# Attention scores of every unit as plain float32, the two heads on two halves of the TensorE rows

## The chip, the cores and the metric

The kernel runs on one core of a Trainium2 chip. The metric is the time of one execution on the device in microseconds (us). A core has TensorE (PE, matrix products; PEld is its weight load), VectorE (DVE), ScalarE (ACT), GpSimd (POOL) and SyncE (SP, which here issues most DMAs). Products are accumulated in PSUM, eight banks of 512 float32 words in each of 128 partitions; everything else lies in SBUF.

## The reference, cut to what matters

Four sequences of 768 tokens, eight heads of 64 go through a sparse attention, and its output through two feed-forward networks. A token attends to the 96 tokens up to itself and to the first 8 tokens.

```python
scores = scale * np.matmul(q, k.transpose(0, 1, 3, 2)) + bias   # bias: -slope * distance
scores = np.where(keep, scores, -1000000000.0)
a = softmax(scores);  x = np.matmul(a, v)
h = (x @ w1) * (x @ w2) @ w3;  x = h @ w_out                    # first network
h = x @ w_in;  out = (h * np.cos(h)) @ w_out2                   # second network
```

## The kernel before, in words

**Units.** The attention is cut into 96 units. A unit is 128 query tokens of one sequence for a pair of heads; its keys are a window of 232 columns (`WIN`): the 128 tokens of the tile, the 96 before it and the 8 global ones. Units run in an order written out by hand, three tiles (`TPB`) of a head pair, then the next pair; four pairs make a block of 384 tokens (`TB`), of which there are eight.

**A unit's steps**, each a function called with the unit's number: load (`a_load` or `a_load_plain`, and `a_load_v` for the values), scores on PE (`a_scores`), bias and row maximum on DVE (`a_max`, L569), exponential on ACT (`a_exp`), the norm on ACT or POOL (`a_norm`), transposition on PE (`a_transpose`) and its copy on ACT (`a_tcopy`), product with the values on PE (`a_values`, L635; from block 1 on for three units at once) and the result's copy (`a_out`).

**Scores in two ways.** Units 0 to 21 (`PLAIN`) are plain float32: both heads' queries and keys lie on partitions 0 to 63, and each head is one product over 64 rows (L541), which the trace shows as two passes. The other 74 units are split: the array is loaded twice, on both halves of the partitions (`a_load`, L496). ACT rounds it to float32r (`a_split_hi`, L517, tile `hh`), and DVE subtracts to get the rests (`a_split_lo`, L524 and L527): the lower halves of the queries' rows hold the value, the upper the rest, and `kl` holds the keys' rests. A head is then two accumulated products over 128 rows (L549, L553), one pass each. The scores of a unit, both heads in one bank, go to one of two buffers of the PSUM pool `p_s`, opened with `bufs` 2 (L285).

**Stages.** First the product W of two weight matrices is built in 16 chunks (L854, plain float32, 512 columns), while the weights of everything are decoded from 64-bit words (`decode`, on ACT at L330 and L332, on DVE at L336, L340, L348) and units 0 to 13 run in between. Then, in 96 slots (`for j`, `for i`), block j goes through the first network: a slot has two groups of 12 matmuls of 384 columns each (`up` or `down`, by `mm3`, L392 to L394), and unit `sl + 14` (`LEAD`) is put between them. In slot order: the load of a unit two or three ahead, `a_scores(n)`, the values of earlier units, the split of unit n + 2, maximum, decoding, exponential, the first group of 12 matmuls, transposition of unit n - 1, norm, the second group of 12. The last 14 slots have no attention. From about 640 us on the second network runs alone (`hidden`, `gate`, `project`).

Within an engine's queue the work is done in program order; loads by SP are issued in the order written, too, and wait there for their buffer.

Of the kernel before, what the change touches and what calls it, by code (L numbers as in the profile page):

```python
# [8 lines left out]
F32 = mybir.dt.float32  # L9
# [4 lines left out]
ALU = mybir.AluOpType  # L14
# [9 lines left out]
LOC, GLB = 96, 8  # L24
NPV = LOC + GLB
WIN = 128 + NPV
QK_W = 2 * 128 + 2 * WIN
TB = 384
NB1 = NT // TB
TPB = TB // 128  # L30
# [4 lines left out]
NB2 = NT // TB2  # L35
M2 = DF2 // 128
LEAD = 14
PLAIN = 22
INV2PI = 0.15915494309189535
C1 = 6.28125  # L40
C2 = 0.0019353071795864769
# [18 lines left out]
def general(ctx, tc, dram, misc, ident, nv, mm_out, packed):  # L60
# [7 lines left out]
    def attention(ctx):  # L68
# [35 lines left out]
        with tc.For_i(0, B, 1) as b:  # L104
            for p in range(NPAIR):
                for e in range(2):
# [5 lines left out]
                    for t in range(nt):  # L112
                        n = bass.ds(b * (nt * NPAIR) + (t // TPB) * UPB + p * TPB + t % TPB, 1)
                        c = slice(t * 128, (t + 1) * 128)
                        k0 = 256 + e * WIN
                        nc.sync.dma_start(
                            out=qt[:, c], in_=a_qk[n, 0:64, e * 128:(e + 1) * 128]
                        )
                        nc.sync.dma_start(out=kt[:, c], in_=a_qk[n, 0:64, k0:k0 + 128])
                        nc.sync.dma_start(out=vt[:, t, :], in_=a_v[n, :, e * 64:(e + 1) * 64])  # L120
                    xo = work.tile([64, S], F32, name="g_x")
                    for t in range(nt):
# [141 lines left out]
def fused(ctx, tc, a_qk, a_v, w3p, wo1p, w1p, w2p, winp, wo2p, n_global, n_local, out):  # L264
# [221 lines left out]
        p, i = divmod(r, TPB)  # L486
        return j, p, i, (TPB * j + i) % (S // 128)

    plain = {}
    qk_raw, v_raw, hh, kl, es, sts, pts, xps, xT = {}, {}, {}, {}, {}, {}, {}, {}, {}  # L490

    def a_load(n):
        if not PLAIN <= n < NU:
            return
        t = attn.tile([128, QK_W], F32, tag="qk", name="qk", bufs=2)
        nc.sync.dma_start(out=t, in_=a_qk[n])  # L496
        qk_raw[n] = t

    def a_load_plain(n, queue=None):

        if not 0 <= n < PLAIN:
            return
        t = plain[n] = attn.tile([128, QK_W], F32R, tag="hh", name="hh")[0:64].bitcast(F32)
        (queue or nc.sync).dma_start(out=t, in_=a_qk[n, 0:64])

    def a_load_v(n):
        if not 0 <= n < NU:
# [2 lines left out]
        nc.sync.dma_start(out=t.rearrange("p a b -> p (a b)"), in_=a_v[n])  # L510
        v_raw[n] = t

    def a_split_hi(n):
        if not PLAIN <= n < NU:
            return
        hh[n] = attn.tile([128, QK_W], F32R, tag="hh", name="hh")
        nc.scalar.copy(out=hh[n], in_=qk_raw[n])  # L517

    def a_split_lo(n):
        if not PLAIN <= n < NU:  # L520
            return
        r, t = qk_raw.pop(n), hh[n]
        kl[n] = attn.tile([128, 2 * WIN], F32R, tag="kl", name="kl")
        nc.vector.tensor_tensor(  # L524
            out=kl[n], in0=r[:, 256:], in1=t[:, 256:].bitcast(F32), op=ALU.subtract
        )
        nc.vector.tensor_tensor(  # L527
            out=t[64:128, :256], in0=r[64:128, :256], in1=t[64:128, :256].bitcast(F32),
            op=ALU.subtract,
        )  # L530

    s_ps = {}

    def a_scores(n):
        if not 0 <= n < NU:
            return
        s_ps[n] = p_s.tile([128, 2, WIN], F32, tag="s", name="s_ps")
        if n in plain:
            t = plain.pop(n)
            for e in range(2):  # L540
                nc.tensor.matmul(  # L541
                    s_ps[n][:, e, :], lhsT=t[:, e * 128:(e + 1) * 128],
                    rhs=t[:, 256 + e * WIN:256 + (e + 1) * WIN], start=True, stop=True,
                )
            return
        t, l = hh.pop(n), kl.pop(n)
        for e in range(2):
            q = t[:, e * 128:(e + 1) * 128]
            nc.tensor.matmul(  # L549
                s_ps[n][:, e, :], lhsT=q, rhs=t[:, 256 + e * WIN:256 + (e + 1) * WIN],  # L550
                start=True, stop=False,
            )
            nc.tensor.matmul(  # L553
                s_ps[n][:, e, :], lhsT=q, rhs=l[:, e * WIN:(e + 1) * WIN],
                start=False, stop=True,
            )

    def a_max(n):
# [187 lines left out]
    with tc.manual_schedule():  # L746
# [81 lines left out]
            for _ in range(n):  # L828
                next(steps_left, None)

        a_load_plain(0, nc.scalar)
        a_scores(0)
        nc.vector.memset(pt_ps, 0.0)
        steps_b = biases(tp)
# [3 lines left out]
        for i in range(21):  # L838
            decode(1)
            if i == 0:  # L840
                a_load_plain(1)
                a_load_v(0)
            if i == 4:
                nv = next(steps_b)
            elif i >= 6:
                dists = dists or next(steps_b)
        W_ps = {}
        for c, (h, k) in enumerate(chunks):
            n = c - 1 if c < 2 * M1 - 1 else -9
            if k == 0:  # L850
                W_ps = {m: p_mm.tile([128, 512], F32, tag="mm", name="mm") for m in range(4)}

            def wmm(m):
                nc.tensor.matmul(  # L854
                    W_ps[m], lhsT=wt["w3", c][:, m * 128:(m + 1) * 128], rhs=wt["wo1", k],
                    start=k == 0, stop=k == M1 - 1,
                )
                if k == M1 - 1:
                    t = wt["W", 4 * h + m] = wts.tile(
                        [128, 2, 512], F32R, tag="Wb" if h else "Wa", name="W", bufs=4  # L860
                    )
                    nc.scalar.copy(out=t[:, 0, :], in_=W_ps[m])
                    nc.vector.tensor_tensor(  # L863
                        out=t[:, 1, :], in0=W_ps[m], in1=t[:, 0, :].bitcast(F32), op=ALU.subtract
                    )

            a_load(n + 3)
            a_load_v(n + 1 if n >= 0 else -1)
            if c < 4:
                bias_heads(*dists, range(2 * c, 2 * c + 2))  # L870
            elif c == 4:
                tp.release()
            if n > 0:
                a_scores(n)
            if n >= 0:
                a_load_plain(n + 2)
            a_values(n - 2)
            a_max(n)
            decode(1)
            a_out(n - 2)  # L880
            a_split_hi(n + 2)
            a_exp(n)
            decode(1)
            a_split_lo(n + 2)
            wmm(0)
            wmm(1)
            if c in (2, 3) or c == 2 * M1 - 1:

                wmm(2)
                wmm(3)  # L890
            a_transpose(n - 1)
            a_tcopy(n - 1)
            a_norm(n, True, lambda: decode(1)) if n >= 0 else decode(2)
            decode(2 if c < 8 else 3)
            if not (c in (2, 3) or c == 2 * M1 - 1):
                wmm(2)
                wmm(3)
# [17 lines left out]
        for j in range(NB1):  # L915
            for i in range(UPB):
# [3 lines left out]
                if last and i == 0:  # L920
                    attn.release()
                    w2p_ = pool("w2p", 6)
                a_load(n + 3)
                if last:
                    if i < 3:
                        late_load("in", i)
# [4 lines left out]
                    if i == 4:  # L931
                        x2_load(0, w2p_, "x2in")
                a_scores(n)
                a_load_plain(n + 2)
                if (n - 2) % TPB == TPB - 1:
                    for u in range(n - 1 - TPB, n - 1):
                        a_values(u)
                if n > LEAD + 1:
                    a_load_v(n - 1)
                a_split_hi(n + 2)  # L940
                if 1 <= i <= M1:
                    up_mult(j, i - 1)
                    up_hi(j, i - 1)
# [9 lines left out]
                    up_lo(j, i - 1)  # L953
                a_exp(n)
                a_out(n - 2)
                a_split_lo(n + 2)
                if i < M1:
                    up(j, i, "a")
                    up_copy(j, i)
# [130 lines left out]
def _layout(q, k, v, w3, w_out, w1, w2, w_in, w_out2):  # L1090

    import numpy as np

    nt = S // 128
    qk = np.zeros((NU, 128, QK_W), np.float32)
    vv = np.zeros((NU, 128, 2, 128), np.float32)
    for n in range(NU):
        j, r = divmod(n, UPB)
        p, i = divmod(r, TPB)
        b, t = divmod(TPB * j + i, nt)  # L1100
        lo = t * 128
        for e in range(2):
            h = 2 * p + e
            for half in (slice(0, 64), slice(64, 128)):
                qk[n, half, e * 128:(e + 1) * 128] = q[b, h, lo:lo + 128].T
                w = qk[n, half, 256 + e * WIN:256 + (e + 1) * WIN]
                w[:, :128] = k[b, h, lo:lo + 128].T
                if t:
                    w[:, 128:128 + LOC] = k[b, h, lo - LOC:lo].T
                    w[:, 128 + LOC:] = k[b, h, :GLB].T  # L1110
            c = slice(e * 64, (e + 1) * 64)
            vv[n, :, 0, c] = v[b, h, lo:lo + 128]
            if t:
                vv[n, :LOC, 1, c] = v[b, h, lo - LOC:lo]
                vv[n, LOC:NPV, 1, c] = v[b, h, :GLB]

    def cols(w):
        kk, f = w.shape[0] // 128, w.shape[1] // 128
        return np.ascontiguousarray(
            w.reshape(kk, 128, f, 128).transpose(2, 1, 0, 3).reshape(f, 128, kk * 128)  # L1120
        )

    def words(w):
        return np.ascontiguousarray(w).view(np.int64)

    w3t = np.ascontiguousarray(w3.T).reshape(M1, 128, 2, 512).transpose(2, 0, 1, 3)
    return {
        "a_qk": qk,
        "a_v": vv.reshape(NU, 128, 256),
        "w3p": words(w3t),  # L1130
        "wo1p": words(w_out.reshape(M1, 128, DM)),
        "w1p": words(cols(w1)),
        "w2p": words(cols(w2)),
        "winp": words(cols(w_in)),
        "wo2p": words(w_out2.reshape(M2, 128, DM)),
    }
# [24 lines left out]
```

## Time and profile before

| | us |
|---|---|
| median of 3 runs | 1170.43 |
| lowest and highest run | 1169.32, 1174.7 |
| the profiled execution | 1168.78 |
| its span | 1167.0 |
| PE busy | 1138.3 |
| weight loads (PEld) busy | 985.5 |
| DVE busy | 753.8 |
| ACT busy | 593.9 |
| POOL busy | 112.3 |

Busy time is time in which an engine had an instruction of the program at work; the engines run beside each other. Matmuls are pipelined: a pass starts before the last one has left the array, so that the distance of two starts says what a pass costs, and its own duration does not. A row of the timeline has the start, the duration, engine, line, operation, tiles (out<-in), shape, and how many instructions are merged in it; a number in brackets is idle time before it and what ended it.

### The profile page before, as it was taken

To read this page: it belongs to the slowest core of one execution; us is meant where nothing else is said; L and a number is where in the kernel's file an instruction comes from. 1 tells how busy PE (TensorE), PEld (TensorE's weight loads), DVE (VectorE), ACT (ScalarE), POOL (GpSimd) and SP (SyncE) were. 2 spreads that over 40 slices of the span, in tenths; PEclk is the share of its full clock that TensorE was granted. 3 is DMA by queue.
4 is the path that set the end of the run, shared out by engine and by line. 5 is a ranking of instruction groups with operands and counts; after the bars stand their busy time and mean duration, and the time that the engine had idled before them with its cause. 6 is when DMAs were issued, how large, how long until landed. Compare 5 with 4: busy or idle time off the path is not lost.

```text
span 1167.0 us, 17288 instructions
## 1 busy us (share of the span) xinstructions
PE 1138.3 (98%) x6178; PEld 985.5 (84%) x6178; DVE 753.8 (65%) x1696; ACT 593.9 (51%) x1309; POOL 112.3 (10%) x197
## 2 busy tenths in 40 slices
PE   5999999999999999999999999999999999999997
PEld 2455899999999999999999888888888888888885
DVE  7797786767676555555344766666666666666664
ACT  6997786666666555555444533333333333333332
POOL 0000001121112111111132300000000000000000
PEclk9899899999999999999999999999999999999999
DMA  8875686575654424343156302002003003000001
GB/s 267 249 227 179 213 298 215 168 222 158 206 169 152 134 88 141 90 151 95 57 173 210 117 1 89 20 1 89 20 1 96 14 1 102 7 1 36 1 1 39
DMA packets 64783, 131.12 MB, mean 112 GB/s; under 512 B 6576, under 2 KB 27312, under 8 KB 64688
## 3 DMA queue, kind: packets, MB, share of 16 engines
q1 hardware_dynamic: 57648, 117.03, 31.2%
q0 software_dynamic: 6528, 12.58, 3.7%
q8 instruction: 51, 0.84, 0.3%
q14 instruction: 44, 0.36, 0.1%
q10 hardware_dynamic: 512, 0.32, 0.1%
HBM read 102.64 MB, written 27.26 MB: 111 GB/s over the span
## 4 chain that ended last, share of the span: by engine, by line
PE 91%; ACT 3%; DMA 2%; DVE 2%; issue 1%; ACTq 0%; SPq 0%; DVEq 0%
PE mm L392 11%; PE mm L394 11%; PE mm L393 11%; PE o_ps L394 7%; PE h_ps L393 7%; PE o_ps L393 7%; PE h_ps L392 7%; PE o_ps L392 7%; PE h_ps L394 7%; PE x_ps L635 3%; PE mm L854 3%; PE pt_ps L608 2%; PE s_ps L553 1%; PE pt_ps L610 1%; PE s_ps L549 1%; DMA raw<-in_winp 1%
## 5 line engine op out<-in xcount | busy, mean ns | idle before, releaser
L1012 ACT ACTIVATE r<-r 128x512 f32<-128x512 f32 x96 | 60.7, 632 | 149.0 <-DVE r L1008 149.0
L1021 ACT CAST g<-r 128x512 fp32r<-128x512 f32 x96 | 59.6, 621 | 139.5 <-DVE r L1017 139.5
L601 POOL TENSOR_SCALAR e<-e,st 128x232 f32<-128x232 f32 x148 | 72.0, 498 | 499.5 <-DVE st L593 479.3
L517 ACT CAST hh<-qk 128x720 fp32r<-128x720 f32 x74 | 58.7, 794 | 118.4 <-PE s_ps L553 113.3
L1014 DVE SCALAR_TENSOR_TENSOR r<-r 128x512 f32<-128x512 f32 x96 | 66.4, 692 | 70.0 <-ACT r L1012 69.9
L1022 DVE TENSOR_TENSOR g<-r,g 128x512 fp32r<-128x512 f32 x96 | 66.5, 692 | 66.0 <-ACT g L1021 66.0
L392 PE MATMUL mm<-xT,wA 128*128 128x384 f32 x256 | 90.6, 354 | 2.3 <-DVE W L863 2.3
L569 DVE CUSTOM_DVE_ANT_0 e<-s_ps,bias 128x232 f32<-128x232 f32 (+1 forms) x192 | 65.5, 378 | 42.3 <-PE s_ps L553 38.9
L580 ACT ACTIVATE e<-e,top 128x232 f32<-128x232 f32 (+1 forms) x192 | 89.3, 468 | 2.3 <-DVE top L569 2.2
L392 PE MATMUL mm<-ab,W 128*128 128x384 f32 x256 | 89.8, 351 | 0.0
L392 PE MATMUL mm<-xT,wB 128*128 128x384 f32 x256 | 89.5, 350 | 0.0
L394 PE MATMUL mm<-xT,wA 128*128 128x384 f32 x256 | 86.9, 340 | 0.0
L393 PE MATMUL mm<-xT,wA 128*128 128x384 f32 x256 | 86.7, 338 | 0.0
L394 PE MATMUL mm<-xT,wB 128*128 128x384 f32 x256 | 86.2, 337 | 0.0
L394 PE MATMUL mm<-ab,W 128*128 128x384 f32 x256 | 86.2, 337 | 0.0
L393 PE MATMUL mm<-ab,W 128*128 128x384 f32 x256 | 85.9, 336 | 0.0
L393 PE MATMUL mm<-xT,wB 128*128 128x384 f32 x256 | 85.8, 335 | 0.0
L1005 DVE SCALAR_TENSOR_TENSOR r<-kt,h_ps 128x512 f32<-128x512 int32 x96 | 65.7, 684 | 28.5 <-ACT kt L1003 28.1
L1003 ACT ACTIVATE kt<-h_ps 128x512 int32<-128x512 f32 x96 | 57.2, 596 | 34.8 <-PE h_ps L394 34.8
L678 DVE TENSOR_TENSOR ab_f<-mm,a_sb 128x384 f32<-128x384 f32 x64 | 35.5, 555 | 55.8 <-PE mm L394 55.8
L1008 DVE SCALAR_TENSOR_TENSOR r<-kt,r 128x512 f32<-128x512 int32 x96 | 66.4, 692 | 3.3
L854 PE MATMUL mm<-wo,w 128*128 128x512 f32 x128 | 63.8, 632 | 4.5 <-DVE wo L348 4.5
(191 smaller groups left out, 3004.3 us busy)
## 6 DMA issues: line engine op xcount, KB each, us to landing
qk<-in_a_qk SPq DMA_DIRECT2D x74, 360.0 KB, 3.1
v<-in_a_v SPq DMA_DIRECT2D x96, 128.0 KB, 2.9
x2s<-x2t SPq DMA_DIRECT2D x32, 384.0 KB, 3.0
raw<-in_w3p SPq DMA_DIRECT2D x16, 512.0 KB, 5.2
raw<-in_winp SPq DMA_DIRECT2D x16, 512.0 KB, 4.3
late_w<-x SPq DMA_DIRECT2D x32, 256.0 KB, 2.1
raw<-in_wo2p SPq DMA_DIRECT2D x16, 512.0 KB, 3.9
raw<-late_w SPq DMA_DIRECT2D x16, 512.0 KB, 4.2
```

The costliest lines, as they stand in the source:

```text
L392: nc.tensor.matmul(ps, lhsT=l_hi, rhs=r_hi, start=first and i == 0, stop=False)
L393: nc.tensor.matmul(ps, lhsT=l_hi, rhs=r_lo, start=False, stop=False)
L394: nc.tensor.matmul(ps, lhsT=l_lo, rhs=r_hi, start=False, stop=last and i == n - 1)
L569: nc.vector.tensor_tensor_reduce(out=es[n][:, e, :w], in0=sp[:, e, :w], in1=bias[:, 2 * p + e, :], scale=-0.125, scalar=3.0e38, op0=ALU.ad ...
L580: nc.scalar.activation(es[n][:, e, :w], es[n][:, e, :w], ACTF.Exp, bias=top[:, n, e:e + 1], scale=-1.0, accum_out=sts[n][:, 0, e:e + 1],)
L601: nc.gpsimd.tensor_scalar(x, x, st[:, 1, e:e + 1], 1.0, ALU.mult, ALU.mult)
L854: nc.tensor.matmul(W_ps[m], lhsT=wt["w3", c][:, m * 128:(m + 1) * 128], rhs=wt["wo1", k], start=k == 0, stop=k == M1 - 1,)
L1005: nc.vector.scalar_tensor_tensor(out=r, in0=kt, scalar=-C1, in1=ps, op0=ALU.mult, op1=ALU.add)
L1008: nc.vector.scalar_tensor_tensor(out=r, in0=kt, scalar=-C2, in1=r, op0=ALU.mult, op1=ALU.add)
L1012: nc.scalar.activation(r, r, ACTF.Sin, scale=0.5)
L1014: nc.vector.scalar_tensor_tensor(out=r, in0=r, scalar=-2.0, in1=r, op0=ALU.mult, op1=ALU.mult)
L1022: nc.vector.tensor_tensor(out=t[:, 1, :], in0=r, in1=t[:, 0, :].bitcast(F32), op=ALU.subtract)
```

## The change

All 96 units are plain. A unit's array has head 0 on partitions 0 to 63 and head 1 on 64 to 127, with 128 columns of queries and 232 of keys, and is loaded once; a head's product runs over its own 64 rows, and so on its own half of the array's rows. Each head's scores go to a bank of their own, in one buffer of two banks in place of two buffers of one. The split is gone, with its tiles. The load has three buffers and is issued two units ahead; the order of a slot is otherwise as it was. The general path and the arrangement of the inputs follow the new layout.

```diff
-QK_W = 2 * 128 + 2 * WIN
+QK_W = 128 + WIN
-PLAIN = 22
...
-    def a_load(n):
-        if not PLAIN <= n < NU:
+    def a_load(n, queue=None):
+
+        if not 0 <= n < NU:
             return
-        t = attn.tile([128, QK_W], F32, tag="qk", name="qk", bufs=2)
-        nc.sync.dma_start(out=t, in_=a_qk[n])
-        qk_raw[n] = t
-
-    def a_load_plain(n, queue=None):
-
-        if not 0 <= n < PLAIN:
-            return
-        t = plain[n] = attn.tile([128, QK_W], F32R, tag="hh", name="hh")[0:64].bitcast(F32)
-        (queue or nc.sync).dma_start(out=t, in_=a_qk[n, 0:64])
+        qk[n] = attn.tile([128, QK_W + 8], F32, tag="qk", name="qk", bufs=3)
+        (queue or nc.sync).dma_start(out=qk[n][:, :QK_W], in_=a_qk[n])
...
-    def a_split_hi(n):
...
-    def a_split_lo(n):
...
     def a_scores(n):
         if not 0 <= n < NU:
             return
-        s_ps[n] = p_s.tile([128, 2, WIN], F32, tag="s", name="s_ps")
...
+        t = qk.pop(n)
+        s_ps[n] = p_s.tile([128, 2, 512], F32, tag="s", name="s_ps", bufs=1)
         for e in range(2):
-            q = t[:, e * 128:(e + 1) * 128]
+            r = slice(e * 64, (e + 1) * 64)
             nc.tensor.matmul(
-                s_ps[n][:, e, :], lhsT=q, rhs=t[:, 256 + e * WIN:256 + (e + 1) * WIN],
-                start=True, stop=False,
-            )
-            nc.tensor.matmul(
-                s_ps[n][:, e, :], lhsT=q, rhs=l[:, e * WIN:(e + 1) * WIN],
-                start=False, stop=True,
+                s_ps[n][:, e, :WIN], lhsT=t[r, :128], rhs=t[r, 128:QK_W], start=True, stop=True
             )
...
-            a_load(n + 3)
...
-                a_load_plain(n + 2)
+                a_load(n + 2)
...
-            a_split_hi(n + 2)
...
-            a_split_lo(n + 2)
...
-                a_load(n + 3)
+                a_load(n + 2)
...
-                a_load_plain(n + 2)
...
-                a_split_hi(n + 2)
...
-                a_split_lo(n + 2)
```

## Rows read from the trace of the kernel before

**Rows 1.** The page: busy us of each engine, share of the span, instructions
```profile
PE 1138.3 (98%) x6178; PEld 985.5 (84%) x6178; DVE 753.8 (65%) x1696; ACT 593.9 (51%) x1309; POOL 112.3 (10%) x197
```
**Rows 2.** Waits of PE, 160 to 571 us: line, releaser, total us, times, longest
```profile
PE x_ps L635 <- ACT pt L618: 0.7, 1, 0.7
```
**Rows 3.** Stretches: length, busy us (count) by engine, granted clock, DMA share, GB/s
```profile
29.70:36.40 6.70, 5.38 (x12) 2.85 (x13) 5.21 (x16) 6.70 (x21) 0.00 (x0) 0.50 1.00 307
...
31.00:92.00 61.00, 60.98 (x236) 31.01 (x237) 50.28 (x144) 55.65 (x143) 0.00 (x0) 0.96 0.76 236
92.00:160.00 68.00, 63.06 (x339) 51.32 (x338) 54.57 (x139) 54.93 (x126) 0.00 (x0) 0.95 0.67 218
160.00:571.00 411.00, 410.26 (x2880) 400.17 (x2879) 260.01 (x802) 249.10 (x635) 71.13 (x146) 1.00 0.48 152
```
**Rows 4.** The chain in order of time: first and last score group on PE
```profile
31.02 1.88 PE s_ps L541 x4
...
88.50 0.98 PE s_ps L541 x4
```
**Rows 5.** Tile qk: the conversion, count, ns min/median/max, first and last start
```profile
L517 ACT CAST hh<-qk x74: 777/794/804, 151.6 to 558.6; 128x720 fp32r<-128x720 f32 x74
```
**Rows 6.** Timeline of PE around the scores of a split unit
```profile
302.23 0.34 PE L394 MATMUL mm<-ab,W 128*128 128x384 f32 x1
...
302.85 0.34 PE L392 MATMUL mm<-ab,W 128*128 128x384 f32 x1
303.03 0.34 PE L393 MATMUL mm<-ab,W 128*128 128x384 f32 x1
```
**Rows 7.** Timeline of PE around the scores of a plain unit
```profile
149.20 0.34 PE L394 MATMUL mm<-xT,wB 128*128 128x384 f32 x1
149.47 1.05 PE L541 MATMUL s_ps<-hh 64*128 64x232 f32 x4
...
150.73 0.34 PE L393 MATMUL mm<-xT,wB 128*128 128x384 f32 x1
```
**Rows 8.** The same unit in narrow windows: its second and fourth pass, its first loads
```profile
149.77 0.36 PE L541 MATMUL s_ps<-hh 64*128 64x232 f32 x1
...
150.16 0.36 PE L541 MATMUL s_ps<-hh 64*128 64x232 f32 x1
...
149.47 0.29 PEld L541 LDWEIGHTS s_ps<-hh 64*128 64x128 f32 x2 [0.25 <-DVE st L590]
```
**Rows 9.** Timeline of PE with values behind the scores: split unit, then plain unit
```profile
312.44 0.34 PE L394 MATMUL mm<-ab,W 128*128 128x384 f32 x1
...
313.15 1.54 PE L635 MATMUL x_ps<-pt,v 128*64 128x128 f32 x24
...
314.91 0.34 PE L393 MATMUL mm<-ab,W 128*128 128x384 f32 x1
...
141.92 0.34 PE L394 MATMUL mm<-xT,wB 128*128 128x384 f32 x1
...
144.92 0.34 PE L393 MATMUL mm<-xT,wB 128*128 128x384 f32 x1
```
**Rows 10.** Tile s_ps: the split units' first passes
```profile
L549 PE MATMUL s_ps<-hh x148: 267/270/274, 161.0 to 570.0; 128*128 128x232 f32 x148
```
**Rows 11.** Timelines of PE and DVE: scores and row maximum (its second half)
```profile
21.15 1.05 PE L541 MATMUL s_ps<-hh 64*128 64x232 f32 x4
...
25.33 0.28 DVE L569 CUSTOM_DVE_ANT_0 e<-s_ps,bias 128x128 f32<-128x128 f32 x1
...
303.47 0.40 DVE L569 CUSTOM_DVE_ANT_0 e<-s_ps,bias 128x232 f32<-128x232 f32 x1
...
307.51 0.27 PE L549 MATMUL s_ps<-hh 128*128 128x232 f32 x1
```
**Rows 12.** Waits of PE, 20 to 32 us
```profile
PE pt_ps L608 <- ACT e L599: 2.7, 1, 2.7
PE s_ps L541 <- DVE wo L340: 1.9, 1, 1.9
```

More of the change, by code (lines that the diff above doesn't have):

```diff
@@ L114, in attention @@
                         c = slice(t * 128, (t + 1) * 128)
-                        k0 = 256 + e * WIN
-                        nc.sync.dma_start(
-                            out=qt[:, c], in_=a_qk[n, 0:64, e * 128:(e + 1) * 128]
-                        )
-                        nc.sync.dma_start(out=kt[:, c], in_=a_qk[n, 0:64, k0:k0 + 128])
+                        r = slice(e * 64, (e + 1) * 64)
+                        nc.sync.dma_start(out=qt[:, c], in_=a_qk[n, r, 0:128])
+                        nc.sync.dma_start(out=kt[:, c], in_=a_qk[n, r, 128:256])
                         nc.sync.dma_start(out=vt[:, t, :], in_=a_v[n, :, e * 64:(e + 1) * 64])
@@ L487, in where @@
         return j, p, i, (TPB * j + i) % (S // 128)
-    plain = {}
-    qk_raw, v_raw, hh, kl, es, sts, pts, xps, xT = {}, {}, {}, {}, {}, {}, {}, {}, {}
-    def a_load(n):
-        if not PLAIN <= n < NU:
+    qk, v_raw, es, sts, pts, xps, xT = {}, {}, {}, {}, {}, {}, {}
+    def a_load(n, queue=None):
+        if not 0 <= n < NU:
             return
-        t = attn.tile([128, QK_W], F32, tag="qk", name="qk", bufs=2)
-        nc.sync.dma_start(out=t, in_=a_qk[n])
-        qk_raw[n] = t
-    def a_load_plain(n, queue=None):
-        if not 0 <= n < PLAIN:
-            return
-        t = plain[n] = attn.tile([128, QK_W], F32R, tag="hh", name="hh")[0:64].bitcast(F32)
-        (queue or nc.sync).dma_start(out=t, in_=a_qk[n, 0:64])
+        qk[n] = attn.tile([128, QK_W + 8], F32, tag="qk", name="qk", bufs=3)
+        (queue or nc.sync).dma_start(out=qk[n][:, :QK_W], in_=a_qk[n])
     def a_load_v(n):
@@ L511, in a_load_v @@
         v_raw[n] = t
-    def a_split_hi(n):
[L514 to L517, printed above, removed]
-    def a_split_lo(n):
[L520 to L530, printed above, removed]
     s_ps = {}
@@ L536, in a_scores @@
             return
-        s_ps[n] = p_s.tile([128, 2, WIN], F32, tag="s", name="s_ps")
-        if n in plain:
-            t = plain.pop(n)
-            for e in range(2):
-                nc.tensor.matmul(
[L542 to L546, printed above, removed]
+        t = qk.pop(n)
+        s_ps[n] = p_s.tile([128, 2, 512], F32, tag="s", name="s_ps", bufs=1)
         for e in range(2):
-            q = t[:, e * 128:(e + 1) * 128]
+            r = slice(e * 64, (e + 1) * 64)
             nc.tensor.matmul(
-                s_ps[n][:, e, :], lhsT=q, rhs=t[:, 256 + e * WIN:256 + (e + 1) * WIN],
-                start=True, stop=False,
-            )
-            nc.tensor.matmul(
-                s_ps[n][:, e, :], lhsT=q, rhs=l[:, e * WIN:(e + 1) * WIN],
-                start=False, stop=True,
+                s_ps[n][:, e, :WIN], lhsT=t[r, :128], rhs=t[r, 128:QK_W], start=True, stop=True
             )
@@ L829, in decode @@
                 next(steps_left, None)
-        a_load_plain(0, nc.scalar)
+        a_load(0, nc.scalar)
         a_scores(0)
@@ L840, in fused @@
             if i == 0:
-                a_load_plain(1)
+                a_load(1)
                 a_load_v(0)
@@ L1103, in _layout @@
             h = 2 * p + e
[L1104 to L1110, printed above, removed]
+            w = qk[n, e * 64:(e + 1) * 64]
+            w[:, :128] = q[b, h, lo:lo + 128].T
+            w[:, 128:256] = k[b, h, lo:lo + 128].T
+            if t:
+                w[:, 256:256 + LOC] = k[b, h, lo - LOC:lo].T
+                w[:, 256 + LOC:] = k[b, h, :GLB].T
             c = slice(e * 64, (e + 1) * 64)
```

## The prediction, made before the changed kernel was run

> **What bounds the kernel now.** I read the shares of busy time first: TensorE (PE) is busy for 98% of the span [rows 1]. That alone proves little, so the waits come next. Between 160 and 571 us, where nearly all split scores lie, PE has one wait, of 0.7 us in 411 us, at the full clock [rows 2, 3]. There its instruction stream is the time: an operation longer by 0.1 us there ends the kernel 0.1 us later, and work taken from the other engines gives nothing. The stage before is different. From 31 to 92 us PE is busy without a gap, yet ACT is busy for 55.65 of 61 us; from 92 to 160 us PE has some 5 us idle [rows 3]. The chain of waits agrees: from 31 to 88 us it runs through PE with every unit's scores in it [rows 4], afterwards through ACT, DVE and the weight loads that decode the late weights. So the change is priced in PE time after 160 us, and with care before.
>
> **What goes away.** Each of the 74 split units loses one ACT conversion (794 ns [rows 5]) and two DVE subtractions, and its load shrinks from 720 to 360 columns. After 160 us PE waits for none of this, so I price it at nothing: the cover is PE's own stream, and since the removed work only makes operands earlier, there is nothing to pay if the cover goes. The first conversion starts at 151.6 us [rows 5], too late to help the stage before.
>
> **What a unit costs PE.** I measure from the start of the last ordinary matmul before the scores to the start of the second one after them, so that the cost of getting in and out is included.
> - Split, now: 303.03 - 302.23 = 0.80 us [rows 6]. Four full-array passes go in at the stream's pace.
> - Plain, now, both heads on the same 64 rows: 150.73 - 149.20 = 1.53 us [rows 7]. The four passes follow each other 0.195 us apart (150.16 - 149.77 is two steps [rows 8]), 0.78 us in all. Two ordinary steps of 0.17 to 0.18 us (the distance of neighbours in rows 6) take 0.35 us. The remaining 0.40 us is the switch: PE pauses and loads the first weights uncovered on the way into 64 rows, and again on the way out.
> - Plain, after: the heads sit on different halves of the rows and in different banks. If the halves run side by side, four steps become two: 1.53 - 2 x 0.195 = 1.14 us. So each former split unit is **0.34 us dearer**, although its array time falls: 0.40 us of switch outweighs it.
>
> That halves run side by side is seen in this trace for halves of the columns only: the values' 24 passes of 128 columns, issued head after head, take 1.54 us [rows 9], where 24 steps scaled from the scores' pace (0.195 x 128 / 232 = 0.108) would take 2.6 us. I take the same for halves of the rows, as the nearest row there is. The far end is no overlap at all, 1.53 us.
>
> Every third slot has the values right behind the scores. They switch the array anyway, so less is added: now 314.91 - 312.44 = 2.47 us, behind a plain unit 144.92 - 141.92 = 3.00 us [rows 9], after it 3.00 - 0.39 = 2.61 us: 0.14 us dearer.
>
> A second place to weigh is the weight load. Two loads of the plain scores start within the first 0.29 us [rows 8], so the second pass's weights go into the same rows while the first pass streams; I therefore add nothing per pass. The Trainium skill, "TensorE: Matmul & The Clock Gate", Part 3, says that a weight load overlaps matmuls in flight only when its row group differs. By that rule each head's second load would stand uncovered, and the sum would be 7.8 us higher; the trace disagrees with it here.
>
> **The sum after 160 us.** The 148 first passes at L549 are 74 units [rows 10]. Of units 22 to 95, every third (22, 25, ... 94) has the values behind it: 25, and 49 have not. 49 x 0.34 + 25 x 0.14 = 16.7 + 3.5 = **+20.2 us**.
>
> **The stage before.** The 22 plain units each save 0.39 us of PE. On the chain these are 11 score groups, 31.02 to 88.50 us [rows 4]: at most -4.3 us. ACT has 61 - 55.65 = 5.35 us free in that stretch [rows 3] and must keep up with a faster PE, so I take half, **-2 us**; the ends are 0 and -4.3 us. Units 14 to 21 lie where PE waits for decoding; their saving turns into longer waits, 0.
>
> **The single score buffer.** Scores now hold both banks at once, so unit n+1's scores wait for unit n's maximum on DVE. After 160 us the maximum is done well before: for the unit at 302.4 us it ends at 303.47 + 0.40 = 303.87 us, and the next scores start at 307.51 us [rows 11]. At the start it is not: unit 1's scores ran at 21.15 us, unit 0's maximum ended at 25.33 + 0.28 = 25.61 us [rows 11]. PE stalls 4.5 us, and W's first products queue behind it. But PE next waits 2.7 us and 1.9 us for ACT and DVE [rows 12], which covers 4.6 us; DVE does not wait for those products there. I take 0; the ends are 0 and +4.5 us. The clock is a second uncertainty: from 29.7 to 36.4 us it is granted at 0.50 (1.2 of 2.4 GHz) after PE's waits [rows 3], and 5.38 us of work at that level loses 2.7 us. Moved idle time can end that or make another, -2.7 to +2.7 us.
>
> Loads keep their place on SP's queue relative to the values' loads, apart from being asked for two units ahead instead of three; a third buffer frees the queue from waiting for DVE's subtraction, and no PE wait in rows 2 is for a load. 0.
>
> **Total:** +20.2 - 2 = +18.2 us. The profiled execution took 1168.78 us (span 1167.0), which gives 1187.0; the median of the runs is 1170.43 us, 1.65 us above it, so in its terms 1188.6, and I say **1188 us**.
>
> **Rivals.**
> 1. *The halves overlap only partly.* If the weights of the two halves load one after the other, each unit pays one more uncovered load, about 149.77 - 149.47 - 0.195 = 0.105 us [rows 7, 8]: 74 x 0.105 = 7.8 us more, 1196 us. For it: the scores load 128 columns per half, the values 64. Against: the values' pace shows both loads and streams paired. Chance 0.08.
> 2. *The change does not do what it says:* the two heads' passes go through one after the other, as they are issued. Then units cost 1.53 us and 3.00 us: 49 x 0.73 + 25 x 0.53 = 49 us, and the early stage saves nothing: about 1219.5 us. For it: the issue order is head 0 complete, then head 1. Against: the values are issued in the same order and overlap. No run here has two halves of the rows at work; the Trainium skill, same page, Part 3, has row tiles start about 4 ns apart. Chance 0.10.
> 3. *Not slower: the switch disappears.* If PE could load the halves' weights under the preceding matmuls and needed no pause, the 0.40 us would go; 49 x 0.40 + 25 x 0.20 = 24.6 us come off (with the values behind, only the way in is new), so 1188.6 - 24.6 = 1164 us. It decides from three quarters of the switch upwards (18.2 of 24.6). For it: a split unit's weights are loaded under the passes before them, its whole unit in 0.80 us. Against: the plain unit pays the whole switch [rows 7], and nothing in the change touches it. The Trainium skill, "TensorEngine Tiling (Array Packing)", Key Properties, says that changing the tiling mode drains the engine; by that rule the switch stays, and the trace agrees. Chance 0.05.
>
> **How the numbers follow.** The forecast has 0.74; 0.03 is left for gains in the early stage that I do not see. The forecast's own ends are 1188.6 - 2.3 - 2.7 = 1183.6 and 1188.6 + 2 + 2.7 + 4.5 = 1198; with rival 1 and part of these on top it reaches 1202. The range 1183 to 1202 us holds both, 0.82. Within 0.5% (about what a measurement of this kernel can tell from no change, 5.9 us) I give 0.05, faster 0.05 with rival 3, slower 0.90.
>
> **What would show each step.** In the changed profile, the stretch from the last ordinary matmul to the second one after should read about 1.14 us without values and 2.61 us with them; 1.53 and 3.00 mean rival 2, 1.25 rival 1, 0.75 rival 3. The score passes should start in pairs a few ns apart. The conversions and subtractions should be gone from ACT and DVE without a wait of PE changing after 160 us. Near 21 us PE should show a wait of some 4.5 us for the maximum, and the shorter waits behind it should have shrunk. I am wrong if PE's stream after 160 us is not longer by about 20 us, or if PE there begins to wait for the maximum, which would say that the single buffer binds.

## The result and the profile after

The changed kernel takes 1184.08 us, median of 4 runs (1183.78 to 1185.93), beside 1171.4 us for the kernel before on the same chips: a ratio of 1.0109, with a 95% interval of 1.0082 to 1.0136. It is 13 us slower; 1188 us was forecast, with a range of 1183 to 1202. The profiled execution took 1183.78 us with a span of 1181.9 us.

The page's busy time, to be held against [rows 1]:

```profile
PE 1150.6 (97%) x6178; PEld 961.9 (81%) x6178; DVE 676.2 (57%) x1548; ACT 547.6 (46%) x1235; POOL 109.9 (9%) x197
```

DVE lost 78 us of work and ACT 46 us, and the kernel became slower. PE, the engine that sets the time, gained 12 us, with the same number of instructions.

The timeline of PE around one unit without values (start, duration, line, tiles, shape, count; the last row is from a window of 10 ns at 308.66 us, when two of the four passes had started):

```profile
308.38 0.34 PE L391 MATMUL mm<-ab,W 128*128 128x384 f32 x1
308.65 0.66 PE L512 MATMUL s_ps<-qk 64*128 64x232 f32 x4
309.25 0.44 PE L389 MATMUL mm<-ab,W 128*128 128x384 f32 x1
309.52 0.34 PE L390 MATMUL mm<-ab,W 128*128 128x384 f32 x1
...
308.65 0.47 PE L512 MATMUL s_ps<-qk 64*128 64x232 f32 x2
```

From the last ordinary matmul to the second one after it is 309.52 - 308.38 = 1.14 us, where [rows 6] has 0.80 us. Two passes had begun by 308.66 us, and passes of one head follow each other 0.195 us apart [rows 8], so these are one of each head: the halves run side by side. What is left in the 1.14 us beside 0.39 us of passes and two ordinary steps is the way into the 64-row tiling and out of it, 0.40 us, as in [rows 7].

The four weight loads of that unit, in one row of PEld's timeline:

```profile
308.65 0.30 PEld L512 LDWEIGHTS s_ps<-qk 64*128 64x128 f32 x4 [0.25 <-issue]
```

The same with the values behind the scores:

```profile
313.83 0.34 PE L391 MATMUL mm<-ab,W 128*128 128x384 f32 x1
314.10 0.66 PE L512 MATMUL s_ps<-qk 64*128 64x232 f32 x4
314.69 1.54 PE L593 MATMUL x_ps<-pt,v 128*64 128x128 f32 x24
...
316.44 0.34 PE L390 MATMUL mm<-ab,W 128*128 128x384 f32 x1
```

That is 2.61 us for the 2.47 us of [rows 9]. Both are medians too: over the 49 units without values the distance is 0.798 us before and 1.138 us after.

The stretches (length, busy us of PE, PEld, DVE, ACT, POOL with counts, granted clock, DMA share, GB/s) answer to [rows 3]:

```profile
31.00:92.00 61.00, 60.43 (x265) 28.78 (x265) 54.03 (x154) 58.66 (x148) 0.00 (x0) 1.00 0.79 244
92.00:160.00 68.00, 60.31 (x355) 51.16 (x354) 54.83 (x141) 55.25 (x132) 0.00 (x0) 0.92 0.69 222
160.00:584.00 424.00, 424.00 (x2829) 378.07 (x2827) 177.69 (x638) 197.75 (x546) 68.69 (x146) 1.00 0.36 112
```

After 160 us PE is busy without a gap, as before, while DVE's and ACT's work there has fallen to 178 and 198 us. In the first stretch the same 61 us now hold 265 passes instead of 236, and ACT is at 58.66 us of 61: the early stage was sped up, and ACT kept pace. Part of this is the clock: it was granted at 0.96 in this stretch before and at 1.00 here.

The waits of PE up to 32 us:

```profile
PE s_ps L512 <- DMA qk<-in_a_qk: 5.6, 1, 5.6
PE mm L812 <- DVE wo L345: 4.7, 1, 4.7
PE s_ps L512 <- issue: 4.5, 1, 4.5
```

The third is new, and the two waits of [rows 12] are gone. It ends at 24.89 us, when unit 0's maximum has ended on DVE (24.49 + 0.29 = 24.78 us). The profile names no releaser for it ("issue"); that it is the single score buffer is shown by the run with one buffer below, which has it too. The timelines of DVE and of PE there:

```profile
24.49 0.29 DVE L527 CUSTOM_DVE_ANT_0 e<-s_ps,bias 128x128 f32<-128x128 f32 x1
...
24.89 0.76 PE L512 MATMUL s_ps<-qk 64*128 64x232 f32 x4 [4.55 <-issue]
```

Where the time went can be read from the starts of the units' scores on PE:

| scores of unit | before, us | after, us | after less before |
|---|---|---|---|
| 2 | 31.02 | 30.98 | 0.0 |
| 3 | 39.01 | 36.08 | -2.9 |
| 14 | 103.14 | 96.75 | -6.4 |
| 23 | 168.71 | 162.85 | -5.9 |
| 95 | 569.79 | 583.91 | +14.1 |

The rows of units 23 and 95, first in the kernel before, then in the changed one:

```profile
168.71 0.27 PE L549 MATMUL s_ps<-hh 128*128 128x232 f32 x1
...
569.79 0.27 PE L549 MATMUL s_ps<-hh 128*128 128x232 f32 x1
...
162.85 0.47 PE L512 MATMUL s_ps<-qk 64*128 64x232 f32 x2
...
583.91 0.47 PE L512 MATMUL s_ps<-qk 64*128 64x232 f32 x2
```

From unit 23 to unit 95 the changed kernel loses 20.0 us, evenly; before unit 23 it had won 5.9 us. The 5.9 us belong to this pair of profiles: the profiled execution of the kernel before (1168.78 us) is 2.6 us under that kernel's median. The medians are 12.7 us apart; with 20.8 us lost from unit 23 to the end (20.0 up to unit 95, 0.8 from there), that leaves some 8 us won before.

### The profile page after: what moved, and what is told of

Its sections match the earlier page's. It is cut to its first block, busy times and chain, and to the rows that moved or that the text cites. A ratio compares the mean times of both kernels' runs of the same rounds, so it can differ in the third digit from the quotient of the medians.

```text
span 1181.9 us, 17049 instructions
## 1 busy us (share of the span) xinstructions
PE 1150.6 (97%) x6178; PEld 961.9 (81%) x6178; DVE 676.2 (57%) x1548; ACT 547.6 (46%) x1235; POOL 109.9 (9%) x197
## 4 chain that ended last, share of the span: by engine, by line
PE 90%; ACT 4%; DVE 2%; DMA 2%; issue 1%; POOL 0%; ACTq 0%; SPq 0%; DVEq 0%; POOLq 0%
PE mm L389 12%; PE mm L391 11%; PE mm L390 11%; PE o_ps L391 7%; PE h_ps L389 7%; PE o_ps L389 7%; PE h_ps L391 7%; PE h_ps L390 7%; PE o_ps L390 7%; PE s_ps L512 4%; PE x_ps L593 3%; PE pt_ps L566 2%; PE mm L812 1%; PE pt_ps L568 1%; ACT s L329 1%; ACT e L538 1%
## 5 line engine op out<-in xcount | busy, mean ns | idle before, releaser
L559 POOL TENSOR_SCALAR e<-e,st 128x232 f32<-128x232 f32 x148 | 69.6, 482 | 516.1 <-DVE st L551 332.9
L389 PE MATMUL mm<-xT,wA 128*128 128x384 f32 x256 | 92.7, 362 | 3.1 <-DVE W L821 3.1
L389 PE MATMUL mm<-xT,wB 128*128 128x384 f32 x256 | 91.9, 359 | 0.0
L391 PE MATMUL mm<-xT,wA 128*128 128x384 f32 x256 | 87.5, 342 | 0.0
L390 PE MATMUL mm<-xT,wA 128*128 128x384 f32 x256 | 86.9, 339 | 0.0
L391 PE MATMUL mm<-xT,wB 128*128 128x384 f32 x256 | 86.6, 338 | 0.0
L390 PE MATMUL mm<-xT,wB 128*128 128x384 f32 x256 | 86.1, 336 | 0.0
L957 DVE SCALAR_TENSOR_TENSOR r<-kt,h_ps 128x512 f32<-128x512 int32 x96 | 65.7, 685 | 28.1 <-ACT kt L955 27.6
L640 ACT CAST ab<-ab_f 128x384 fp32r<-128x384 f32 x64 | 32.9, 513 | 104.7 <-DVE ab_f L636 104.7
L512 PE MATMUL s_ps<-qk 64*128 64x232 f32 x384 | 64.2, 411 | 10.6 <-DMA qk<-in_a_qk 5.6
```

The lines of the kernel that those rows point to most:

```text
L389: nc.tensor.matmul(ps, lhsT=l_hi, rhs=r_hi, start=first and i == 0, stop=False)
L390: nc.tensor.matmul(ps, lhsT=l_hi, rhs=r_lo, start=False, stop=False)
L391: nc.tensor.matmul(ps, lhsT=l_lo, rhs=r_hi, start=False, stop=last and i == n - 1)
L512: nc.tensor.matmul(s_ps[n][:, e, :WIN], lhsT=t[r, :128], rhs=t[r, 128:QK_W], start=True, stop=True)
L559: nc.gpsimd.tensor_scalar(x, x, st[:, 1, e:e + 1], 1.0, ALU.mult, ALU.mult)
L957: nc.vector.scalar_tensor_tensor(out=r, in0=kt, scalar=-C1, in1=ps, op0=ALU.mult, op1=ALU.add)
```

## The experiments

Seven runs were made: four new kernels, each timed against the kernel before, and three kernels profiled once more.

**Both heads on the same rows, all units plain.** The kernel before with one number changed:

```diff
-PLAIN = 22
+PLAIN = 96
```

> The kernel before with all 96 units plain, both heads on the same 64 rows and in one bank; the split is gone here too. Theory (a plain unit pays a switch of 0.40 us, and halves of the rows halve its four passes): units cost 1.53 us without and 3.00 us with the values behind them, 0.39 us more than in the changed kernel; up to unit 22 nothing moves. 49 x 0.73 + 25 x 0.53 = 49 us over the kernel before, about 1220 us. Rival (the placing of the heads matters little, the time comes from giving up the split): near the changed kernel's 1184 us, at most 1190.

Measured: 1218.2 us, ratio 1.040 (1.0382 to 1.0419). The timeline of PE around a unit without values:

```profile
317.33 0.34 PE L394 MATMUL mm<-ab,W 128*128 128x384 f32 x1
317.60 1.05 PE L541 MATMUL s_ps<-hh 64*128 64x232 f32 x4
318.58 0.44 PE L392 MATMUL mm<-ab,W 128*128 128x384 f32 x1
318.86 0.34 PE L393 MATMUL mm<-ab,W 128*128 128x384 f32 x1
```

318.86 - 317.33 = 1.53 us, and 3.00 us with the values. This kernel has given up the split as the changed one has, and it is 34 us slower than that one: 27.3 us between the scores of units 23 and 95 (72 x 0.39 would be 28.1 us) and most of the rest in the early stage, where it has no gain. So leaving out the split gave nothing on PE's path, and the halves of the rows are worth 0.39 us a unit. The changed kernel also gives each head a bank of its own; no run has the halves of the rows with one bank, so the two are not told apart.

**All rows of the array, no change of tiling.** The changed kernel with zeros in the other head's rows of the queries:

```diff
-QK_W = 128 + WIN
+QK_W = 256 + WIN
...
-            r = slice(e * 64, (e + 1) * 64)
             nc.tensor.matmul(
-                s_ps[n][:, e, :WIN], lhsT=t[r, :128], rhs=t[r, 128:QK_W], start=True, stop=True
+                s_ps[n][:, e, :WIN], lhsT=t[:, e * 128:(e + 1) * 128], rhs=t[:, 256:QK_W],
+                start=True, stop=True,
             )
...
```

What follows in the diff arranges the inputs to match.

> The changed kernel with each head's 64 rows of queries filled up with 64 rows of zeros, so that a product runs over all 128 rows of the array and the tiling never changes; four float32 passes one after the other, otherwise the same. Theory (the 0.40 us are the price of going to another tiling and back): the switch is gone, the passes do not overlap, 4 x 0.195 + 0.35 = 1.13 us without the values; with them the way into the column halves is still paid, 2.47 - 0.44 + 0.78 = 2.81 us. That is 25 x 0.20 = 5 us over the changed kernel after unit 22, about 1189 us. Rival (the 0.40 us belong to float32 passes among float32r ones, whatever the rows): 1.53 us and 3.00 us a unit, about 1213 us.

Measured: 1189.35 us, ratio 1.0149 (1.0132 to 1.0166). A unit without and one with the values:

```profile
306.62 0.34 PE L391 MATMUL mm<-ab,W 128*128 128x384 f32 x1
306.79 0.94 PE L511 MATMUL s_ps<-qk 128*128 128x232 f32 x4
307.41 0.50 PE L389 MATMUL mm<-ab,W 128*128 128x384 f32 x1
307.75 0.34 PE L390 MATMUL mm<-ab,W 128*128 128x384 f32 x1
...
317.44 0.34 PE L391 MATMUL mm<-ab,W 128*128 128x384 f32 x1
...
318.49 1.54 PE L593 MATMUL x_ps<-pt,v 128*64 128x128 f32 x24
...
320.24 0.34 PE L390 MATMUL mm<-ab,W 128*128 128x384 f32 x1
```

The scores start 0.17 us after the last ordinary matmul, at the stream's own pace, where the halves start 0.27 us after it. 307.75 - 306.62 = 1.13 us: four float32 passes in a row cost as much as two steps and a change of tiling. With the values it is 320.24 - 317.44 = 2.80 us instead of 2.61 us. The 0.40 us are the price of the tiling, not of float32 passes among others; the rival's 1.53 us does not occur. The whole is 5.3 us slower than the changed kernel, as expected, but that agreement is partly luck: between units 23 and 95 it takes 423.91 us, only 2.9 us more than the changed kernel's 421.06 us, and 2.7 us were lost before unit 23.

**One score buffer in the kernel before.**

```diff
-        s_ps[n] = p_s.tile([128, 2, WIN], F32, tag="s", name="s_ps")
+        s_ps[n] = p_s.tile([128, 2, WIN], F32, tag="s", name="s_ps", bufs=1)
```

> The kernel before with one score buffer instead of two; nothing else. Theory (the wait of unit 1's scores for unit 0's maximum moves PE's idle time, and the stretch at the lower clock behind it gets shorter): PE waits some 4 us at 21 us, unit 2's scores start near 31.0 us as before, unit 3's near 36 us instead of 39; the end comes about 3 us earlier, 1168.5 us. Rival (the early gain is from the shorter scores alone): unit 3's scores at 39 us or later, 1171 to 1173 us.

Measured: 1169.81 us in 10 runs, ratio 0.9985 (0.9974 to 0.9995). The wait came (3.8 us), but what was expected of it only in part: unit 2's scores start at 33.14 us and not near 31.0, unit 3's at 38.55 us, neither at 36 as the theory had it nor at 39 or later as the rival had it. The stretch at the lower clock moved forward, to 24.2 to 31.1 us, and did not get shorter:

```profile
24.30:31.00 6.70, 5.23 (x8) 2.67 (x9) 6.51 (x21) 5.87 (x18) 0.00 (x0) 0.50 0.89 291
```

The end is some 2 us earlier, but this pair of profiles does not show where: at unit 23 (169.75 us) it is 1.0 us behind that of the kernel before, which was faster than all its timed runs. In the second pair, below, one buffer is 4.1 us ahead there (169.57 against 173.66 us). The one thing that is settled is that the single buffer costs nothing here.

**The first 22 units on halves of the rows, the rest split.** The kernel before, with the plain units' data in the new arrangement:

```diff
-        t = plain[n] = attn.tile([128, QK_W], F32R, tag="hh", name="hh")[0:64].bitcast(F32)
-        (queue or nc.sync).dma_start(out=t, in_=a_qk[n, 0:64])
+        t = plain[n] = attn.tile([128, QK_W], F32R, tag="hh", name="hh")[:, :128 + WIN].bitcast(F32)
+        (queue or nc.sync).dma_start(out=t, in_=a_qp[n])
...
-        s_ps[n] = p_s.tile([128, 2, WIN], F32, tag="s", name="s_ps")
+        s_ps[n] = p_s.tile([128, 2, 512], F32, tag="s", name="s_ps", bufs=1)
...
+                r = slice(e * 64, (e + 1) * 64)
                 nc.tensor.matmul(
-                    s_ps[n][:, e, :], lhsT=t[:, e * 128:(e + 1) * 128],
-                    rhs=t[:, 256 + e * WIN:256 + (e + 1) * WIN], start=True, stop=True,
+                    s_ps[n][:, e, :WIN], lhsT=t[r, :128], rhs=t[r, 128:], start=True, stop=True
                 )
...
```

What follows in the diff makes the new array and lets the split products write to the wider buffer.

> The two put together: units 0 to 21 as in the changed kernel (heads on halves of the rows), units 22 to 95 split as before, one score buffer of two banks throughout. Theory (the changed kernel is 20 us dearer from unit 22 on and some 6 us quicker before): unit 22 starts some 5 us earlier than before, its successors cost 0.80 us and 2.47 us, 1171.4 - 6 = 1165.5 us, better than both kernels. Rival (ACT's and DVE's split work, which begins at 150 us, takes the early gain back, since those engines set the pace there): unit 30 starts within 1 us of the kernel before, 1170 to 1172 us.

Measured: **1165.41 us, ratio 0.9953 (0.9935 to 0.9971)**: faster than both kernels. Timeline of PE at units 3, 14 and 23, and around a split unit:

```profile
37.21 0.47 PE L542 MATMUL s_ps<-hh 64*128 64x232 f32 x2
...
97.85 0.47 PE L542 MATMUL s_ps<-hh 64*128 64x232 f32 x2
...
163.26 0.27 PE L549 MATMUL s_ps<-hh 128*128 128x232 f32 x1
...
296.78 0.34 PE L394 MATMUL mm<-ab,W 128*128 128x384 f32 x1
296.95 0.27 PE L549 MATMUL s_ps<-hh 128*128 128x232 f32 x1
...
297.58 0.34 PE L393 MATMUL mm<-ab,W 128*128 128x384 f32 x1
```

Unit 23 starts 168.71 - 163.26 = 5.4 us earlier than before, and the split work of ACT and DVE behind it takes nothing back: a split unit costs 297.58 - 296.78 = 0.80 us, also with one score buffer.

**Three profiles once more**, to see what of the early gain stays the same in another execution. The kernels are those above, unchanged.

> The kernel before, unchanged, profiled a second time. Theory (how long PE stays at the lower clock behind its early waits differs between executions of one program, while the shorter scores are worth the same in each): from unit 3's scores to unit 14's 64.1 us again, to 0.2 us; unit 3's start may move by up to 3 us. Rival (the place and length of that stretch belong to the program): the lower clock again from about 29.7 to 36.5 us, unit 3's scores within 0.5 us of 39.0 us.

> The changed kernel, unchanged, profiled a second time. Theory (as for the kernel before): from unit 3's scores to unit 14's 60.7 us again, to 0.2 us; the first stretch at the lower clock may last 6.8 us instead of 3.4, and unit 3's scores then start near 37.5 us instead of 36.1. Rival (the stretch belongs to the program): again 3.4 us long, unit 3 within 0.5 us of 36.1 us.

> The kernel before with one score buffer, unchanged, profiled a second time. Theory (the stretch differs between executions): from unit 3's scores to unit 14's 64.1 us; unit 3's start may be up to 2 us earlier than 38.55 us, with a first stretch of 3.4 us instead of 6.9. Rival (the stretch belongs to the program): 38.55 us to 0.5 us.

Measured: 1173.63, 1186.23 and 1169.26 us. Starts of the scores in us, and the first stretch at the lower clock after 20 us:

| | unit 3 | unit 14 | 3 to 14 | lower clock |
|---|---|---|---|---|
| before | 39.01 | 103.14 | 64.13 | 29.7 to 36.5 |
| before, again | 40.14 | 104.27 | 64.13 | 31.2 to 38.0 |
| one buffer | 38.55 | 102.68 | 64.13 | 24.2 to 31.1 |
| one buffer, again | 38.88 | 103.00 | 64.12 | 24.7 to 31.6 |
| after | 36.08 | 96.75 | 60.67 | 25.3 to 28.7 |
| after, again | 37.13 | 97.74 | 60.61 | 23.7 to 30.6 |
| first 22 on halves | 37.21 | 97.85 | 60.64 | 23.8 to 30.6 |

The two starts behind the 64.13 us of the kernel before (those of the first 22 on halves are shown above):

```profile
39.01 0.46 PE L541 MATMUL s_ps<-hh 64*128 64x232 f32 x1
...
103.14 0.46 PE L541 MATMUL s_ps<-hh 64*128 64x232 f32 x1
```

The column that matters is the third: 64.1 us with both heads on the same rows, 60.6 us on halves, whatever the buffers. That is 3.5 us, the same in every execution. The stretch in front moves: the changed kernel once had half of it, the next time all, and its unit 3 was 1 us later. For the kernel before the length came again, but 1.5 us later, and unit 3 was 1.1 us later, outside the rival's 0.5 us; for one buffer unit 3 came again within 0.5 us, as the rival says. So neither theory holds for all kernels. Halves also gain something in front of unit 3 where the stretch is the same: with a full one from about 24 to 31 us, unit 3 starts at 37.1 and 37.2 us on halves, at 38.6 and 38.9 us with one buffer and the same rows.

Behind unit 14 executions of one kernel differ more than the kernels do: from there to unit 23 the kernel before takes 65.57 and 69.39 us, the changed one 66.11 and 67.61 us. From unit 23 to unit 95 nothing varies: 401.08 and 401.05 us before, 421.06 us both times after.

## Why the prediction was right

- **PE's stream is the time after 160 us: right.** No wait of PE was added there, the one of 0.7 us before went, and 78 us less on DVE and 46 us less on ACT in the whole run brought nothing there.
- **A unit's cost: right to the hundredth.** 1.14 us and 2.61 us were forecast and measured. 20.2 us was the sum for units 22 to 95; the units between the scores of 23 and 95 have 48 x 0.34 + 24 x 0.14 = 19.7 us of it, and 20.0 us was lost there. With the values a unit became 0.15 us dearer, as the medians have 2.46 us before. Halves of the rows overlap as halves of the columns do, and the switch of 0.40 us is the tiling's: without a change of tiling it is gone, as the run on all rows shows.
- **No uncovered load for the second pass: right.** The 1.14 us leave no room for it. All four loads of the unit above lie between 308.65 and 308.95 us, beside the first two passes. The rule of the Trainium skill that was weighed against it ("TensorE: Matmul & The Clock Gate", Part 3) would have made the units 0.1 us dearer, 1.25 us; the 1.14 us of the changed kernel disagree with it, too.
- **The single buffer: right in the end, in part by luck.** The wait of 4.5 us at unit 1 came as said, and unit 2's scores started at the same time as before (30.98 us). But the later waits did not simply cover it: with one buffer alone, unit 2 started 2.1 us later than before (33.14 us), and in the second profile of the changed kernel at 32.10 us. The same start fell together with a stretch at the lower clock of half the length.
- **The stage before: too small.** "I take half, **-2 us**" of at most 4.3 us, because ACT "must keep up with a faster PE". ACT did: it was busy for 58.66 us of 61. Units 3 to 14 gained 3.5 us, not 2. A further 2 to 3 us came before unit 3, from shorter scores there and from the moved and partly shorter stretch at the lower clock, which was counted as an uncertainty and not as a gain. Units 14 to 21 were given 0, and in the first pair of profiles 0.5 us was lost from unit 14 to 23. So -5.9 us stands in the place of -2.
- **From the profiled execution to the median: too much.** 1.65 us was added; the changed kernel's median is 0.3 us above its profile, while the kernel before's turned out 2.6 us above its own.

In the prediction's sum, 1168.78 + 20.8 - 5.9 + 0.3 gives 1184.0 us. The forecast of 1188 us was some 4 us too high, and the result lies 1.1 us above the lower end of its range, because the early stage came out near the best that the forecast allowed.

Rivals 1 to 3 fall: units cost neither 1.25 us, nor 1.53 us (that is the kernel with the same rows), nor 0.75 us, and the two heads' passes start in pairs, within 10 ns.

What stays open is why the lower clock lasts half as long in some executions, how the gain before unit 3 divides between the clock and the shorter scores, and what makes the stage between units 14 and 23 vary by up to 3.8 us in one kernel; no run took these apart.

## What to carry to other kernels

Price a product on a busy PE as a stretch of its stream, from the last ordinary matmul before to the second one after, not as the sum of its passes: here two heads side by side took less array time than the split, and lost, because the way into another tiling and back cost 0.40 us, as much as the overlap saved. Such a tiling pays where the alternative changes the tiling as well, as in the first 22 units, and against zero-filled rows where its neighbour changes it anyway, as the values do (2.61 against 2.80 us). Work taken from engines off the path was worth nothing here, since the path's own engine had no wait for them.

## What had not been expected of the hardware

Filling half of the array with zeros was as fast as using its halves at once (1.13 and 1.14 us a unit), since the one avoids the switch and the other the waiting in line. The prediction had not weighed this; the sum made ahead of that run gave it. And between 20 us and the last few us, the run on all rows had the lower clock only once, from 23.1 to 29.9 us, where the changed kernel had it four times in one profile (25.3, 100.4, 117.5 and 138.0 us, 3.4 us each) and three times in the other (23.7, 102.2 and 139.8 us); so the difference can't be put down to the rows alone. The later ones cost nothing that can be seen: from unit 14 to unit 23 the changed kernel takes 66.11 us with three of them, the run on all rows 66.29 us with none.
